# A small input as 128 rows of 64 bytes, its statistics by matmul, and a query picked by a register, in a decode block with grouped-query attention

## The chip, the cores and the metric

The kernel runs on one core of a Trainium2 chip. Its time is the device time of one execution in microseconds. A core has five engines with instruction streams of their own: TensorE (PE, matrix multiplications into PSUM), VectorE (DVE), ScalarE (ACT), GpSimd (POOL) and SyncE (SP). They meet only by semaphores. Transfers between the main memory and the on-chip memory (SBUF, 128 partitions) are done by 16 DMA engines. SP and ACT each issue transfers into a DMA queue of their own; in the profile queue 1 is SP's and queue 10 is ACT's. A transfer that has landed raises a semaphore by 16.

## The reference

One token (a decode step) for a batch of two. The input is normalized, and the result is the input plus an attention over a long cache plus a feed-forward layer, both of the normalized input. Everything is 32-bit floating point.

```python
B, Sq, D = 2, 1, 1024
Hq, Hkv, Sk, Dh = 32, 4, 32768, 128
F = 3584

xn = (x - mean(x)) / sqrt(var(x) + 1e-5)          # over the last axis, 1024 numbers
q  = (xn @ wq) -> 32 heads of 128                 # wq 1024 x 4096
k, v = caches (2, 4, 32768, 128), each head used by 8 query heads
o  = softmax(q k^T * 128**-0.5) v
A  = o @ wo                                       # wo 4096 x 1024
Bf = silu(xn @ w1) @ w2                           # w1 1024 x 3584, w2 3584 x 1024
out = x + A + Bf
```

The caches are 268 MB of the 331 MB that are read; the weights are the rest.

## The kernel before, in words

All large operands stream through two buffers of 8 MiB, `bufA` and `bufB` (128 partitions of 64 KB). SP issues the loads in a fixed order, alternating the buffers: `wq[0]`, `wq[1]`, `w1b`, `w1a`; then for each of 8 turns (4 key heads by 2 batch entries) the two halves of the keys `kt` and the two halves of the values `v0`, `v1`; then `wo[0]`, `wo[1]`, `w2a`, `w2b`. Ahead of a load SP waits until TensorE has finished with the buffer's last content: the semaphore `freed`, which VectorE raises in `relay` (line 199) when TensorE's progress count `turn_sem` says so. The `load` helper is at line 167.

Each buffer's content is multiplied by TensorE as 32 groups of matmuls with weights of 32 columns from a small tile `wtA` or `wtB` (line 107 records all matmuls). TensorE runs one loop over pairs of buffers (`te_loop`, `te_more`, line 372 on). Before it uses a buffer it takes two tokens: `ld`, that the buffer has landed, and `tok`, that the small weight tile is ready. Between the pairs it does small matmuls that the softmax needs: with a matrix of ones it sums over partitions, with the identity it transposes.

The start is this. SP issues `wq[0]` (line 110). GpSimd clears the tile `xs` (line 113) and one large tile `blank` (line 114), out of which several smaller tiles are cut that have to begin as zeros. After the first clearing ACT issues the transfer `x8` into `xs` (line 116): 8 rows of 4 KB, the two input rows in four rotations, on every sixteenth partition. After the second it issues `x`, 4 rows of 2 KB, into `xres` (line 118): the residual that is added at the end. SP waits for `x8` to land (line 119, semaphore `ldx`), then issues `wq[1]` (line 120). VectorE takes mean and variance with its statistics instructions (lines 139 to 143), the reciprocal of the square root with one square root on ACT and a Newton step (lines 146 to 151), normalizes 256 columns and transposes them in blocks of 32 (lines 152 and 153) into `xT`. ACT spreads `xT` over `wtA` and GpSimd over `wtB` (lines 161 to 164); with these TensorE can begin `wq[0]`.

The query vectors come out of `wq` and lie in `tqs`. In each turn ACT copies the 8 query columns of that turn into `qcur` (`query`, line 226), GpSimd clears the weight tile and places them in it (`stage`, line 296), the keys are multiplied, VectorE finds the maxima and subtracts them (`attend`, line 259), ACT takes exponentials into the weight tiles (line 236), the values are multiplied, and the normalized result `onew` is copied by ACT into `oT` (line 238); the next copy into `qcur` follows it. VectorE and GpSimd run their 8 turns as a loop with a register as counter (lines 309 to 317).

At the end GpSimd sums partial results and the residual `xres` (lines 334 to 340; the wait for the residual's landing is at line 335), TensorE adds the last pieces of `w2b` one by one as they land, ACT copies the sum out of PSUM (line 246) and SP stores it (line 345).

```python
sp.dma_start(buf[0], wq[0]).then_inc(ld[0], 16)
...
A.dma_start(xs[::16, :], x8).then_inc(ldx, 16)
act.wait(z)
A.dma_start(xres[0:64:16, :], x).then_inc(ldr, 16)
sp.wait_ge(ldx, 16)
sp.dma_start(buf[1], wq[1]).then_inc(ld[1], 16)
```

Of the kernel before, what the change touches and what calls it, by code (L numbers as in the profile page):

```python
# [5 lines left out]
ALU = mybir.AluOpType  # L6
AX = mybir.AxisListType

B, HQ, HKV, SK, DH, D, F = 2, 32, 4, 32768, 128, 1024, 3584
P = 128  # L10
REP = HQ // HKV
W = 16384
NC = SK // W
KT = D // P
FT = F // P
QW = D // 4
CUT = 3 * QW // 4
LOOPS = HKV * B
STEPS = 4 + 4 * LOOPS + 4
PAIRS = STEPS // 2  # L20
EPS = 1e-5
# [27 lines left out]
        self.eng.sem_inc(token, -n)  # L49


def gqa_plus_mlp_kernel(nc, x, x8, kt, v0, v1, wq, wo, w1a, w1b, w2a, w2b, out):


    pe, dve, act, pool = (Stream(nc, e, n) for e, n in
                          ((nc.tensor, "pe"), (nc.vector, "dve"), (nc.scalar, "act"), (nc.gpsimd, "pool")))
    sp, T, V, A, G = nc.sync, nc.tensor, nc.vector, nc.scalar, nc.gpsimd
# [6 lines left out]
    def sb(name, *shape):  # L64
        return nc.alloc_sbuf_tensor(name, shape, F32).ap()
# [5 lines left out]
    ld, more, tok = ([sem(f"{n}{k}") for k in "AB"] for n in ("ld", "more", "tok"))  # L71
    ldx, ldr, done, turn_sem, self_sem = (sem(n) for n in ("ldx", "ldr", "done", "marks", "self"))
    freed, subbed, normed, tq, pself = (sem(n) for n in ("freed", "subbed", "normed", "tq", "pself"))
    trm, tgd, tls, tob = (sem(n) for n in ("trm", "tgd", "tls", "tob"))
    last = [sem(f"last{i}") for i in range(5)]

    wt = [sb(n, P, 32, 32) for n in ("wtA", "wtB")]
    st = [sb(f"st{c}", P, 1024) for c in range(NC)]
    xs, xT = sb("xs", P, D), sb("xT", P, KT, 32)
    stats, mv, ln = sb("stats", P, 2, V.BN_STATS_DIM), sb("mv", P, 2), sb("ln", P, 6)  # L80
    ev = [sb(f"ev{i}", P, 1024) for i in range(4)]
    sums = [sb(f"sum{i}", P, 512) for i in range(4)]
    tqs = [sb(f"tq{i}", P, 16, 32) for i in range(2)]
    pre, sig, rsig = sb("pre", P, FT, 32), sb("sig", P, FT, B), sb("rsig", P, FT, B)
    qcur, onew = sb("qcur", P, REP), sb("onew", P, REP)
    ones = sb("ones", P, P)
    blank, used = sb("blank", P, P + 32 + 160 + 3 * REP + 1024 + 32 * (HQ + FT)), [0]

    def zeroed(*shape):
        n = shape[0] * (shape[1] if len(shape) > 1 else 1)  # L90
        lo = used[0]
        used[0] += n
        t = blank[:, lo:lo + n]
        return t.rearrange("p (a m) -> p a m", m=shape[1]) if len(shape) > 1 else t

    ident, sel, fold, rm, lsum, gd, ob, xres = (zeroed(n) for n in (P, 32, 160, REP, REP, REP, 512, 512))
    oT, hT = zeroed(HQ, 32), zeroed(FT, 32)
    rest, ob1, ot = sb("rest", P, 512), sb("ob1", P, 512), sb("ot", P, QW)
    mx, ls = sb("mx", P, NC, REP), sb("ls", P, NC, REP)
    gm, gmax, rl = sb("gm", REP, 1), sb("gmax", P, 1, REP), sb("rl", P, REP)  # L100
# [2 lines left out]
    smA, smB = bank("smA"), bank("smB")  # L103
    acc = bank("acc")[:, :QW]

    def mm(o, lhsT, rhs, start=True, stop=True):
        return T.matmul(o, lhsT, rhs, start=start, stop=stop)  # L107
# [2 lines left out]
    sp.dma_start(buf[0], wq[0]).then_inc(ld[0], 16)  # L110


    z_x = pool.mark(G.memset(xs, 0.0))
    z = pool.mark(G.memset(blank, 0.0))
    act.wait(z_x)
    A.dma_start(xs[::16, :], x8).then_inc(ldx, 16)
    act.wait(z)
    A.dma_start(xres[0:64:16, :], x).then_inc(ldr, 16)
    sp.wait_ge(ldx, 16)
    sp.dma_start(buf[1], wq[1]).then_inc(ld[1], 16)  # L120

# [1 line left out]
    t = pool.mark(G.affine_select(out=ident, in_=ident, compare_op=ALU.not_equal, fill=1.0, base=0,  # L123
                                  pattern=[[-1, P]], channel_multiplier=1))
    pool.wait(t)
    halves = fold[:, 32:].rearrange("p (a m) -> p a m", m=64)[:, :, :32]
    t = pool.mark(G.tensor_add(halves, *(ident[:, 64 * g:64 * g + 64].rearrange("p (a m) -> p a m", m=32)
                                         for g in range(2))))
    pool.wait(t)
    G.tensor_add(sel, halves[:, 0], halves[:, 1]).then_inc(tob, 1)  # L130
    t = pool.mark(G.memset(ones, 1.0))
    pool.pass_on(tls, 1, t)
    for s in (trm, tgd):
        G.sem_inc(s, 1)
    for s in more:
        G.sem_inc(s, 16 * (PAIRS - 1))


    dve.wait((ldx, 16))
    for i in range(2):  # L140
        t = dve.mark(V.bn_stats(stats[:, i, :], xs[:, i * 512:(i + 1) * 512]))
    dve.wait(t)
    t = dve.mark(V.bn_aggr(mv, stats))
    var, std, y0, t0, t1, rstd = (ln[:, i:i + 1] for i in range(6))
    dve.wait(t)
    t = dve.mark(V.tensor_scalar_add(var, mv[:, 1:2], EPS))
    act.wait(t)
    t = act.mark(A.activation(std, var, AF.Sqrt))
    for f in (lambda: V.reciprocal(y0, std), lambda: V.tensor_mul(t0, y0, y0), lambda: V.tensor_mul(t1, t0, var),
              lambda: V.tensor_scalar(t0, t1, -0.5, 1.5, op0=ALU.mult, op1=ALU.add),  # L150
              lambda: V.tensor_mul(rstd, y0, t0),
              lambda: V.tensor_scalar(xs[:, :256], xs[:, :256], mv[:, 0:1], rstd, op0=ALU.subtract, op1=ALU.mult),
              lambda: V.transpose(xT.rearrange("p k m -> p (k m)"), xs[:, :256])):
        dve.wait(t)
        t = dve.mark(f())
    i_xT = t

    def spread_x(copy, to):
        return copy(to.rearrange("p (k q) m -> p k q m", q=4), xT[:, :, None, :].to_broadcast([P, KT, 4, 32]))

    act.wait(i_xT)
    spread_x(A.copy, wt[0]).then_inc(tok[0], 1)
    pool.wait(i_xT)
    spread_x(G.tensor_copy, wt[1]).then_inc(tok[1], 1)


    def load(k, dst, src, s, n):
# [7 lines left out]
    for it in range(LOOPS):  # L175
        h, b = divmod(it, B)
# [12 lines left out]
    for n in range(4):  # L189
        act.wait((freed, n + 1))  # L190
        t = act.mark(A.copy(ev[n], ps[n % 2]))  # L191
# [10 lines left out]
    relay(2)  # L202
    for n in range(2):
        dve.wait(read[n])
        i_q = dve.mark(V.transpose(tqs[n].rearrange("p c m -> p (c m)"), sums[n]))  # L205
    relay(5)
    relay(6)
    dve.wait(read[2])
# [4 lines left out]
    t = dve.mark(V.transpose(pre[:, :16].rearrange("p t m -> p (t m)"), sums[3]))  # L213

    act.wait(t)
    t = act.mark(A.activation(sig, pre[:, :, ::16], AF.Exp, scale=-1.0))
    for f in (lambda: V.tensor_scalar_add(sig, sig, 1.0), lambda: V.reciprocal(rsig, sig),
              lambda: V.tensor_mul(hT[:, :, ::16], pre[:, :, ::16], rsig)):
        dve.wait(t)
        t = dve.mark(f())  # L220
# [2 lines left out]
    V.sem_inc(turn_sem, -8)  # L223


    def query(it):
        h, b = divmod(it, B)
        A.copy(qcur, tqs[h // 2][:, REP * (h % 2):REP * (h % 2) + REP, 16 * b]).then_inc(tq, 1)

    act.wait(i_q)  # L230
    query(0)
    for it in range(LOOPS):
        h, b = divmod(it, B)
        for c in range(NC):
            act.wait((subbed, NC * it + c + 1))
            A.activation(wt[c].rearrange("p e m -> p (e m)"), st[c], AF.Exp, scale=SCALE).then_inc(tok[c], 1)  # L236
        act.wait((normed, it + 1))
        i_oT = act.mark(A.copy(oT[:, REP * h:REP * (h + 1), 16 * b], onew))  # L238
        if it + 1 < LOOPS:
            query(it + 1)  # L240
    outs = []
    for n in range(3):
        act.wait((freed, STEPS - 3 + n))
        outs.append(act.mark(A.copy(ev[n], ps[n % 2])))
    act.wait((pe, 2))
    i_ot = act.mark(A.copy(ot, acc))  # L246


# [10 lines left out]
    def attend():  # L259
# [33 lines left out]
        V.sem_inc(self_sem, -at[0])  # L293
        V.sem_inc(turn_sem, -8)

    def stage():
        G.wait_ge(tq, 1)
        G.sem_inc(tq, -1)  # L298
        for c in range(NC):
            G.memset(wt[c], 0.0).then_inc(pself, 1)  # L300
            G.wait_ge(pself, c + 1)
            for a in range(2):
                o = bass.AP(tensor=wt[c].tensor, offset=wt[c].offset + 512 * a,
                            ap=[wt[c].ap[0], [136, 4], [32, 4], [1, REP]])
                m = G.tensor_copy(o, qcur[:, None, None, :].to_broadcast([P, 4, 4, REP]))
            m.then_inc(tok[c], 1)
        G.sem_inc(pself, -2)

    turns = [(V, attend, V.alloc_register("ve_turn")), (G, stage, G.alloc_register("po_turn"))]
    for eng, f, reg in turns:  # L310
        eng.reg_mov(reg, 0)
        eng.br("turns")
    with nc.body("turns", valid_engines=[V.engine, G.engine]):
        for eng, f, reg in turns:
            f()
            eng.reg_add(reg, reg, 1)
            eng.br_lt(reg, LOOPS, on_true="turns", on_false="after")
    nc.switch_bb("after")
    for n in (1, 2, 5):
        relay(n)  # L320

    for c in range(NC):
        if c == 0:
            pool.wait(i_oT)
        G.tensor_copy(wt[c].rearrange("p (t d) m -> p t d m", d=2),
                      oT[:, 16 * c:16 * c + 16, None, :].to_broadcast([P, 16, 2, 32])).then_inc(tok[c], 1)
    for s in (trm, tgd):
# [4 lines left out]
        G.tensor_copy(wt[c][:, :2 * n].rearrange("p (t d) m -> p t d m", d=2),  # L332
                      hT[:, 16 * c:16 * c + n, None, :].to_broadcast([P, n, 2, 32])).then_inc(tok[c], 1)
    t = pool.mark(G.tensor_add(ev[0], ev[0], ev[1]))
    pool.wait(t, (ldr, 16))
    t = pool.mark(G.tensor_add(ev[0][:, :512], ev[0][:, :512], xres))
    pool.wait(t, outs[2])
    t = pool.mark(G.tensor_add(ev[0], ev[0], ev[2]))
    pool.wait(t)
    t = pool.mark(G.tensor_add(rest, ev[0][:, :512], ev[0][:, 512:]))  # L340
    dve.wait(t, (pe, 1))
    V.tensor_add(ob, rest, ps[1][:, :512]).then_inc(tob, 1)  # L342

    sp.wait_ge(act.sem, i_ot[1])
# [51 lines left out]
    with nc.body("te_far", valid_engines=engine):  # L396
        T.reg_mov(pair, 0)
        T.reg_mov(half, 0)
        T.br("te_loop")
    nc.switch_bb("te_rest")  # L400

# [62 lines left out]
```

## Time and profile before

| | |
|---|---|
| time, median of 3 runs | 773.19 us (773.11 to 773.69) |
| profiled execution | 772.86 us, of which the span between first and last instruction is 771.6 us |
| read from main memory | 331.39 MB, 430 GB/s over the span |
| busy: PE, DVE, ACT, POOL | 386.7, 142.4, 30.9, 45.0 us |
| SP's queue (1) | 6928 packets, 331.37 MB |
| ACT's queue (10) | 24 packets, 0.04 MB |

Busy times are sums over an engine's instructions. Waiting, issuing a transfer and register work are not counted. The profile also lists for each queue the packets that the DMA engines moved (a packet is one contiguous piece, or the few bytes that raise a semaphore), for each issue the time until its data had landed, and for each wait what ended it. Time that an engine idles matters only where the end of the program hangs on it.

### The profile page before, as it was taken

How to read it: one execution, taken by the hardware profiler on the slowest of the kernel's cores; microseconds unless marked ns; L12 is line 12 of the kernel's file. 1: busy time of each engine (PE TensorE's matmuls, PEld its weight loads, DVE VectorE, ACT ScalarE, POOL GpSimd, SP SyncE). 2: the span in 40 equal slices, each digit the busy share in tenths (PEclk: the TensorE clock that was granted, in tenths of full speed). 3: DMA queues.
4: the chain of work that ended last, by engine and by line, in shares of the span. 5: the costliest groups of instructions: out<-in, count | busy, mean ns of one | idle time of the engine just before them, and what ended most of it. 6: DMA issues, size and time to landing. Idle time of an engine off the chain costs nothing. (4 is left out here: it accounts for less than half of the span.)

```text
span 771.6 us, 6137 instructions
## 1 busy us (share of the span) xinstructions
PE 386.7 (50%) x2702; PEld 120.1 (16%) x2702; DVE 142.4 (18%) x174; ACT 30.9 (4%) x45; POOL 45.0 (6%) x71
## 2 busy tenths in 40 slices
PE   0454554464555454554464555454554464555476
PEld 0111111121111111111121111111111121111122
DVE  1000113111311131113111311131113111311000
ACT  1000101000100010001000100000001000000000
POOL 3000200010001000100000001000100000001021
PEclk9977767767767767767767767767767767767789
DMA  9999999999999999999999999999999999999997
GB/s 384 435 435 435 435 435 435 435 435 435 435 435 435 435 435 435 435 435 435 435 431 435 431 435 435 435 435 435 435 431 428 425 425 428 425 435 435 435 435 327
DMA packets 6954, 331.44 MB, mean 430 GB/s; under 512 B 780, under 2 KB 924, under 8 KB 1448
## 3 DMA queue, kind: packets, MB, share of 16 engines
q1 hardware_dynamic: 6928, 331.37, 99.4%
q10 hardware_dynamic: 24, 0.04, 0.0%
q8 instruction: 1, 0.02, 0.0%
q14 instruction: 1, 0.01, 0.0%
HBM read 331.39 MB, written 0.02 MB: 430 GB/s over the span
## 5 line engine op out<-in xcount | busy, mean ns | idle before, releaser
L107 PE MATMUL xy<-bufB,wtB 128*32 128x512 f32 x1248 | 177.7, 733 | 196.5 <-PEq L49 196.5
L107 PE MATMUL xy<-bufA,wtA 128*32 128x512 f32 x1280 | 182.4, 733 | 118.7 <-PEq L49 118.7
L107 PEld LDWEIGHTS xy<-bufB,wtB 128*32 128x32 f32 x1248 | 48.9, 132 | 325.3 <-issue 325.2
L107 PEld LDWEIGHTS xy<-bufA,wtA 128*32 128x32 f32 x1280 | 50.1, 132 | 234.6 <-issue 234.6
L262 DVE STREAM_TRANSPOSE st<-xy 128x1024 f32<-128x1024 f32 x16 | 20.0, 1250 | 237.1 <-PE xy L107 237.1
L300 POOL MEMSET wtA<- 128x1024 f32 x8 | 7.6, 951 | 525.7 <-POOLq L298 525.7
L264 DVE TENSOR_REDUCE mx<-st 128x8 f32<-128x1024 f32 x16 | 31.7, 1980 | 0.6
L283 DVE TENSOR_TENSOR ob<-ob,xy 128x512 f32<-128x512 f32 x8 | 5.5, 687 | 127.8 <-PE xy L107 127.8
L277 DVE COPY ob<-xy 128x512 f32<-128x512 f32 x8 | 5.5, 691 | 93.1 <-PE xy L107 93.1
L236 ACT ACTIVATE wtA<-st 128x1024 f32<-128x1024 f32 x8 | 8.5, 1057 | 315.7 <-DVE st L275 315.7
L107 PE MATMUL smA<-blank 128*8 128x128 f32 x20 | 4.2, 295 | 30.3 <-PEq L49 30.3
L107 PE MATMUL smA<-blank,ones 128*128 128x8 f32 x18 | 3.9, 288 | 30.6 <-PEq L49 30.6
L275 DVE TENSOR_TENSOR st<-st,gmax 128x1024 f32<-128x1024 f32 x16 | 18.9, 1220 | 0.3
L280 DVE TENSOR_REDUCE ls<-wtA 128x8 f32<-128x1024 f32 x8 | 15.8, 1972 | 0.0
L286 DVE TENSOR_REDUCE ls<-wtB 128x8 f32<-128x1024 f32 x8 | 15.8, 1972 | 0.0
L238 ACT COPY blank<-onew 128x8 f32<-128x8 f32 x8 | 1.6, 204 | 285.3 <-DVE onew L292 285.3
L107 PE MATMUL smB<-blank 128*128 128x8 f32 x72 | 12.3, 299 | 0.0
L107 PEld LDWEIGHTS smB<-blank 128*128 128x128 f32 x72 | 11.8, 248 | 0.0
L342 DVE TENSOR_TENSOR blank<-rest,xy 128x512 f32<-128x512 f32 x1 | 0.7, 687 | 55.5 <-PE acc L107 55.5
L107 PEld LDWEIGHTS smA<-blank,ones 128*128 128x128 f32 x18 | 3.3, 229 | 38.5 <-issue 38.5
L196 POOL TENSOR_TENSOR sum<-ev 128x512 f32<-128x512 f32 x4 | 5.0, 1260 | 67.7 <-ACT ev L191 67.7
L205 DVE STREAM_TRANSPOSE tq<-sum 128x512 f32<-128x512 f32 x2 | 1.4, 712 | 39.2 <-PE xy L107 37.5
(63 smaller groups left out, 98.4 us busy)
## 6 DMA issues: line engine op xcount, KB each, us to landing
bufA<-in_w2a SPq DMA_DIRECT2D x2, 4096.0 KB, 24.2
bufA<-in_w1b SPq DMA_DIRECT2D x1, 6144.0 KB, 25.0
bufB<-in_w2b SPq DMA_DIRECT2D x1, 3072.0 KB, 16.7
bufB<-in_w2b SPq DMA_DIRECT2D x3, 512.0 KB, 20.4
bufB<-in_w2b SPq DMA_DIRECT2D x1, 1024.0 KB, 18.8
bufB<-in_w2b SPq DMA_DIRECT2D x1, 384.0 KB, 21.7
bufA<-in_kt SPq DMA_DIRECT2D x8, 29.2
bufB<-in_kt SPq DMA_DIRECT2D x8, 29.1
```

The source lines that it names most:

```text
L107: return T.matmul(o, lhsT, rhs, start=start, stop=stop)
L196: read.append(pool.mark(G.tensor_add(sums[n], ev[n][:, :512], ev[n][:, 512:])))
L236: A.activation(wt[c].rearrange("p e m -> p (e m)"), st[c], AF.Exp, scale=SCALE).then_inc(tok[c], 1)
L238: i_oT = act.mark(A.copy(oT[:, REP * h:REP * (h + 1), 16 * b], onew))
L262: t = mine(V.transpose(st[c], ps[c]))
L264: t = mine(V.tensor_reduce(mx[:, c, :], e8[c].rearrange("p n m -> p m n"), AX.X, ALU.max))
L275: V.tensor_sub(e8[c], e8[c], gmax.to_broadcast([P, 128, REP])).then_inc(subbed, 1)
L277: t = mine(V.tensor_copy(ob1, ps[0][:, :512]))
L280: mine(V.tensor_reduce(ls[:, 0, :], w8[0], AX.X, ALU.add))
L283: t = mine(V.tensor_add(ob1, ob1, ps[1][:, :512]))
L286: t = mine(V.tensor_reduce(ls[:, 1, :], w8[1], AX.X, ALU.add))
L300: G.memset(wt[c], 0.0).then_inc(pself, 1)
```

## The change

- **The input.** `x8` and the clearing of `xs` go. The input comes as `xk`, 128 rows of 64 bytes, one row for each partition (8 numbers of each of the two batch entries). ACT issues it as its first instruction, without a wait. SP still waits for it ahead of `wq[1]`.
- **Mean and variance.** VectorE sums each partition's 8 numbers; TensorE multiplies with a matrix of ones, which gives the sum over partitions on every partition. The mean is subtracted, the squares are summed in the same way, and the reciprocal square root follows as before, now on two columns. The result goes straight into `xT`, which is now part of `blank`. GpSimd spreads `xT` over both weight tiles.
- **The query.** ACT copies all query columns once into `qall`, in the order of the turns. GpSimd's `stage` reads its 8 columns at a place given by its loop register, which now steps by 8. Its signal in each turn is the copy into `oT`.
- **The residual.** It comes in three transfers of 128, 128 and 256 columns with 10, 12 and 14 rows; in the prepared array the 4 rows of the residual stand at rows 0, 2, 4 and 6, and the others are zero. The wait counts to 48.
- TensorE's progress count `pe` starts two higher, so the later waits on it do too.

```diff
-    z_x = pool.mark(G.memset(xs, 0.0))
+    A.dma_start(xs.rearrange("p k b -> p (k b)"), xk).then_inc(ldx, 16)
     z = pool.mark(G.memset(blank, 0.0))
-    act.wait(z_x)
-    A.dma_start(xs[::16, :], x8).then_inc(ldx, 16)
+    i_ones = pool.mark(G.memset(ones, 1.0))
     act.wait(z)
-    A.dma_start(xres[0:64:16, :], x).then_inc(ldr, 16)
+    for lo, hi, n in ((0, 128, 10), (128, 256, 12), (256, 512, 14)):
+        A.dma_start(xres[:8 * n:8, lo:hi], x[:n, lo:hi]).then_inc(ldr, 16)
     sp.wait_ge(ldx, 16)
     sp.dma_start(buf[1], wq[1]).then_inc(ld[1], 16)
...
     dve.wait((ldx, 16))
-    for i in range(2):
-        t = dve.mark(V.bn_stats(stats[:, i, :], xs[:, i * 512:(i + 1) * 512]))
...
+    i_s1 = dve.mark(V.tensor_reduce(s1, xs.rearrange("p k b -> p b k"), AX.X, ALU.add))
+    dve.wait((pe, 1))
+    t = dve.mark(V.scalar_tensor_tensor(xc, wide(smA[:, :B]), -1.0 / D, xs, op0=ALU.mult, op1=ALU.add))
+    for f in (lambda: V.tensor_mul(sq, xc, xc),
+              lambda: V.tensor_reduce(s2, sq.rearrange("p k b -> p b k"), AX.X, ALU.add)):
+        dve.wait(t)
+        t = dve.mark(f())
+    i_s2 = t
+    dve.wait((pe, 2))
+    t = dve.mark(V.tensor_scalar(var, smB[:, :B], 1.0 / D, EPS, op0=ALU.mult, op1=ALU.add))
...
+    dve.wait(t)
+    i_xT = dve.mark(V.tensor_mul(xT[:, :, ::16], xc, wide(t1)))
...
-    act.wait(i_xT)
-    spread_x(A.copy, wt[0]).then_inc(tok[0], 1)
     pool.wait(i_xT)
-    spread_x(G.tensor_copy, wt[1]).then_inc(tok[1], 1)
+    for k in range(2):
+        spread_x(G.tensor_copy, wt[k]).then_inc(tok[k], 1)
...
-    def query(it):
-        h, b = divmod(it, B)
-        A.copy(qcur, tqs[h // 2][:, REP * (h % 2):REP * (h % 2) + REP, 16 * b]).then_inc(tq, 1)
-
     act.wait(i_q)
-    query(0)
+    A.copy(qall.rearrange("p (h b) m -> p h b m", b=B),
+           tqs[:, :, ::16].rearrange("p (h m) b -> p h b m", m=REP)).then_inc(tq, 1)
...
     def stage():
-        G.wait_ge(tq, 1)
-        G.sem_inc(tq, -1)
+        pool.take(tq)
+        q = qall.rearrange("p i m -> p (i m)")[:, bass.ds(G.snap(at_q), REP)]
...
-                m = G.tensor_copy(o, qcur[:, None, None, :].to_broadcast([P, 4, 4, REP]))
+                m = G.tensor_copy(o, q[:, None, None, :].to_broadcast([P, 4, 4, REP]))
...
-    pool.wait(t, (ldr, 16))
+    pool.wait(t, (ldr, 48))
...
+        pe.wait(i_ones, i_s1)
+        pe.mark(mm(smA[:, :B], ones, s1))
+        pe.wait(i_s2)
+        pe.mark(mm(smB[:, :B], ones, s2))
         T.br("te_loop")
```

More of the change, by code (lines that the diff above doesn't have):

```diff
@@ L49, in take, with gqa_plus_mlp_kernel @@
         self.eng.sem_inc(token, -n)
-def gqa_plus_mlp_kernel(nc, x, x8, kt, v0, v1, wq, wo, w1a, w1b, w2a, w2b, out):
+def gqa_plus_mlp_kernel(nc, xk, x, kt, v0, v1, wq, wo, w1a, w1b, w2a, w2b, out):
     pe, dve, act, pool = (Stream(nc, e, n) for e, n in
@@ L78, in gqa_plus_mlp_kernel @@
     st = [sb(f"st{c}", P, 1024) for c in range(NC)]
-    xs, xT = sb("xs", P, D), sb("xT", P, KT, 32)
-    stats, mv, ln = sb("stats", P, 2, V.BN_STATS_DIM), sb("mv", P, 2), sb("ln", P, 6)
+    xs, xc, sq = (sb(n, P, KT, B) for n in ("xs", "xc", "sq"))
+    ln = sb("ln", P, 7, B)
     ev = [sb(f"ev{i}", P, 1024) for i in range(4)]
     sums = [sb(f"sum{i}", P, 512) for i in range(4)]
-    tqs = [sb(f"tq{i}", P, 16, 32) for i in range(2)]
+    tqs, qall = sb("tqs", P, 32, 32), sb("qall", P, LOOPS, REP)
     pre, sig, rsig = sb("pre", P, FT, 32), sb("sig", P, FT, B), sb("rsig", P, FT, B)
-    qcur, onew = sb("qcur", P, REP), sb("onew", P, REP)
+    onew = sb("onew", P, REP)
     ones = sb("ones", P, P)
-    blank, used = sb("blank", P, P + 32 + 160 + 3 * REP + 1024 + 32 * (HQ + FT)), [0]
+    blank, used = sb("blank", P, P + 32 + 160 + 3 * REP + 1024 + 32 * (KT + HQ + FT)), [0]
     def zeroed(*shape):
@@ L96, in gqa_plus_mlp_kernel @@
     ident, sel, fold, rm, lsum, gd, ob, xres = (zeroed(n) for n in (P, 32, 160, REP, REP, REP, 512, 512))
-    oT, hT = zeroed(HQ, 32), zeroed(FT, 32)
+    xT, oT, hT = zeroed(KT, 32), zeroed(HQ, 32), zeroed(FT, 32)
     rest, ob1, ot = sb("rest", P, 512), sb("ob1", P, 512), sb("ot", P, QW)
@@ L130, in gqa_plus_mlp_kernel @@
     G.tensor_add(sel, halves[:, 0], halves[:, 1]).then_inc(tob, 1)
-    t = pool.mark(G.memset(ones, 1.0))
-    pool.pass_on(tls, 1, t)
-    for s in (trm, tgd):
+    for s in (tls, trm, tgd):
         G.sem_inc(s, 1)
@@ L136, in gqa_plus_mlp_kernel @@
         G.sem_inc(s, 16 * (PAIRS - 1))
+    s1, s2, var, std, y0, t0, t1 = (ln[:, i] for i in range(7))
+    wide = lambda t: t[:, None, :].to_broadcast([P, KT, B])
     dve.wait((ldx, 16))
-    for i in range(2):
[L141 to L146, printed above, removed]
+    i_s1 = dve.mark(V.tensor_reduce(s1, xs.rearrange("p k b -> p b k"), AX.X, ALU.add))
[8 more added lines that the diff above has]
+    t = dve.mark(V.tensor_scalar(var, smB[:, :B], 1.0 / D, EPS, op0=ALU.mult, op1=ALU.add))
     act.wait(t)
@@ L150, in gqa_plus_mlp_kernel @@
               lambda: V.tensor_scalar(t0, t1, -0.5, 1.5, op0=ALU.mult, op1=ALU.add),
-              lambda: V.tensor_mul(rstd, y0, t0),
-              lambda: V.tensor_scalar(xs[:, :256], xs[:, :256], mv[:, 0:1], rstd, op0=ALU.subtract, op1=ALU.mult),
-              lambda: V.transpose(xT.rearrange("p k m -> p (k m)"), xs[:, :256])):
+              lambda: V.tensor_mul(t1, y0, t0)):
         dve.wait(t)
         t = dve.mark(f())
-    i_xT = t
+    dve.wait(t)
+    i_xT = dve.mark(V.tensor_mul(xT[:, :, ::16], xc, wide(t1)))
     def spread_x(copy, to):
         return copy(to.rearrange("p (k q) m -> p k q m", q=4), xT[:, :, None, :].to_broadcast([P, KT, 4, 32]))
-    act.wait(i_xT)
-    spread_x(A.copy, wt[0]).then_inc(tok[0], 1)
     pool.wait(i_xT)
-    spread_x(G.tensor_copy, wt[1]).then_inc(tok[1], 1)
+    for k in range(2):
+        spread_x(G.tensor_copy, wt[k]).then_inc(tok[k], 1)
     def load(k, dst, src, s, n):
@@ L204, in gqa_plus_mlp_kernel @@
         dve.wait(read[n])
-        i_q = dve.mark(V.transpose(tqs[n].rearrange("p c m -> p (c m)"), sums[n]))
+        i_q = dve.mark(V.transpose(tqs[:, 16 * n:16 * n + 16].rearrange("p c m -> p (c m)"), sums[n]))
     relay(5)
@@ L237, in gqa_plus_mlp_kernel @@
         act.wait((normed, it + 1))
-        i_oT = act.mark(A.copy(oT[:, REP * h:REP * (h + 1), 16 * b], onew))
-        if it + 1 < LOOPS:
-            query(it + 1)
+        A.copy(oT[:, REP * h:REP * (h + 1), 16 * b], onew).then_inc(tq, 1)
     outs = []
@@ L244, in gqa_plus_mlp_kernel @@
         outs.append(act.mark(A.copy(ev[n], ps[n % 2])))
-    act.wait((pe, 2))
+    act.wait((pe, 4))
     i_ot = act.mark(A.copy(ot, acc))
@@ L294, in attend @@
         V.sem_inc(turn_sem, -8)
+    at_q = G.alloc_register("at_q")
     def stage():
-        G.wait_ge(tq, 1)
-        G.sem_inc(tq, -1)
+        pool.take(tq)
+        q = qall.rearrange("p i m -> p (i m)")[:, bass.ds(G.snap(at_q), REP)]
         for c in range(NC):
@@ L304, in stage @@
                             ap=[wt[c].ap[0], [136, 4], [32, 4], [1, REP]])
-                m = G.tensor_copy(o, qcur[:, None, None, :].to_broadcast([P, 4, 4, REP]))
+                m = G.tensor_copy(o, q[:, None, None, :].to_broadcast([P, 4, 4, REP]))
             m.then_inc(tok[c], 1)
         G.sem_inc(pself, -2)
-    turns = [(V, attend, V.alloc_register("ve_turn")), (G, stage, G.alloc_register("po_turn"))]
-    for eng, f, reg in turns:
+    turns = [(V, attend, V.alloc_register("ve_turn"), 1), (G, stage, at_q, REP)]
+    for eng, f, reg, step in turns:
         eng.reg_mov(reg, 0)
@@ L313, in gqa_plus_mlp_kernel @@
     with nc.body("turns", valid_engines=[V.engine, G.engine]):
-        for eng, f, reg in turns:
+        for eng, f, reg, step in turns:
             f()
-            eng.reg_add(reg, reg, 1)
-            eng.br_lt(reg, LOOPS, on_true="turns", on_false="after")
+            eng.reg_add(reg, reg, step)
+            eng.br_lt(reg, step * LOOPS, on_true="turns", on_false="after")
     nc.switch_bb("after")
@@ L323, in gqa_plus_mlp_kernel @@
         if c == 0:
-            pool.wait(i_oT)
+            G.wait_ge(tq, 1)
         G.tensor_copy(wt[c].rearrange("p (t d) m -> p t d m", d=2),
@@ L340, in gqa_plus_mlp_kernel @@
     t = pool.mark(G.tensor_add(rest, ev[0][:, :512], ev[0][:, 512:]))
-    dve.wait(t, (pe, 1))
+    dve.wait(t, (pe, 3))
     V.tensor_add(ob, rest, ps[1][:, :512]).then_inc(tob, 1)
@@ L426, in lay @@
         return np.ascontiguousarray(np.asarray(a).reshape(shape).transpose(order)).reshape(to)
-    xr = np.asarray(A_x).reshape(B, D)
+    x_ = np.asarray(A_x).reshape(B, D)
+    spaced = np.zeros((14, 512), x_.dtype)
+    spaced[:8:2] = lay(x_, (B, 2, 512), (1, 0, 2), (4, 512))
     v = np.asarray(A_v_cache).reshape(B, HKV, NC, W, DH)
@@ L441 @@
     arrays = {
-        "x": np.ascontiguousarray(xr.reshape(B, 2, 512).transpose(1, 0, 2)).reshape(4, 512),
-        "x8": np.stack([np.roll(xr, -QW * g, axis=1) for g in range(4)]).reshape(8, D),
+        "xk": lay(x_, (B, 4, KT, 32), (1, 3, 2, 0), (P, KT * B)),
+        "x": spaced,
         "kt": lay(A_k_cache, (B, HKV, NC, W, DH), (0, 1, 2, 4, 3), (B, HKV, NC, P, W)),
```

## The prediction

> **What bounds the kernel now.** I read first the page's slices, queues and chain, then the waits of SP's DMA queue, then the order of time at the start.
>
> ```profile
> span 771.6 us, 6137 instructions
> GB/s 384 435 435 435 435 435 435 435 435 435 435 435 435 435 435 435 435 435 435 435 431 435 431 435 435 435 435 435 435 431 428 425 425 428 425 435 435 435 435 327
> DMA packets 6954, 331.44 MB, mean 430 GB/s; under 512 B 780, under 2 KB 924, under 8 KB 1448
> q1 hardware_dynamic: 6928, 331.37, 99.4%
> q10 hardware_dynamic: 24, 0.04, 0.0%
> q8 instruction: 1, 0.02, 0.0%
> DMA 3%; PE 2%; SPq 0%; ACT 0%; issue 0%; DVEq 0%
> bufA<-in_kt SPq DMA_DIRECT2D x8, 29.2
> bufA<-in_wq SPq DMA_DIRECT2D x1, 22.5
> bufB<-in_wq SPq DMA_DIRECT2D x1, 31.7
> ...
> SPq L170 <- DVEq L44: 719.7, 38, 21.0
> SPq L120 <- DMA xs<-in_x: 9.8, 1, 9.8
> ```
>
> Queue 1, SP's bulk transfers, holds the 16 DMA engines for 99.4% of the span. The slices run at 435 GB/s except the first, the last and a few at 421 to 431, so the kernel is a transfer of 331 MB with a start and an end around it. An 8 MiB load takes 8.39 MB / 435 GB/s = 19.3 us, but from issue to landing a load of `kt` takes 29.2 us: it is queued 29.2 - 19.3 = 9.9 us ahead of need. SP's long wait of 719.7 us costs nothing for that reason. An edit matters if it makes a bulk load late by more than this cover, or if it touches the start or the end.
>
> The start, in order of time (start us, length us, engine, line), then the DMA queues cut into short windows. In each window the GB/s line has 40 slices, a number is what began in that slice, and a queue row is packets, MB, share.
>
> ```profile
> 0.74 0.37 SPq L110 DMA_DIRECT2D bufA<-in_wq  x1
> 1.71 1.15 ACTq L116 DMA_DIRECT2D xs<-in_x  x1
> 4.49 0.53 ACTq L118 DMA_DIRECT2D blank<-in_x  x1
> 10.90 0.33 SPq L120 DMA_DIRECT2D bufB<-in_wq  x1
> 10.91 1.29 DVE L141 BATCH_NORM_STATS2 stats<-xs 128x6 f32<-128x512 f32 x2 [10.91 <-DMA xs<-in_x]
> 14.79 1.04 ACT L159 COPY wtA<-xT 128x1024 f32<-128x1024 f32 x1 [1.93 <-DVE xT L153]
> 14.82 1.04 POOL L159 COPY wtB<-xT 128x1024 f32<-128x1024 f32 x1 [8.96 <-DVE xT L153]
> 23.55 8.59 PE L107 MATMUL xy<-bufA,wtA 128*32 128x512 f32 x64 [23.55 <-PEq L49]
> 32.25 0.68 SPq L170 DMA_DIRECT2D bufA<-in_w1b  x1
> 42.90 9.15 PE L107 MATMUL xy<-bufB,wtB 128*32 128x512 f32 x64 [10.76 <-PEq L49]
> ```
>
> Windows 0 to 4.6 us (its GB/s line), 7 to 9.6 us, 9.6 to 12 us (their queue rows), and 21.8 to 23 us (its GB/s line):
>
> ```profile
> GB/s 0 0 0 0 0 0 0 0 0 0 0 0 0 0 0 2849 2992 570 1710 570 0 0 0 0 570 0 0 0 0 0 0 0 0 0 0 0 0 0 0 0
> ...
> q1 hardware_dynamic: 16, 1.05, 93.7%
> q10 hardware_dynamic: 8, 0.03, 3.1%
> ...
> q1 hardware_dynamic: 16, 1.05, 101.2%
> q10 hardware_dynamic: 8, 0.00, 0.2%
> ...
> GB/s 0 2185 4369 0 0 0 4369 0 6554 4369 0 2185 2185 2185 0 2185 0 0 0 0 0 0 0 0 0 0 0 2185 0 0 0 0 0 2185 0 0 0 0 0 0
> ```
>
> A window of some 2.5 us holds 16 packets of queue 1 with 1.05 MB, so 64 KB each, one per engine: `wq[0]` (128 rows of 64 KB) is 8 such rounds. Queue 10 is ACT's. `x8` (8 rows) appears there as 8 data packets in one round (0.03 MB) and 8 semaphore packets (0.00 MB) in the next, though a semaphore packet is tiny. So while `wq[0]` is in the rings, queue 10 gets **one packet per engine and round**, even for packets of one transfer. That is why 32 KB issued at 1.71 us releases SP only at 10.90 us. It costs nothing today: the last round of `wq[0]` ends between 21.83 us (slice 1 of the last line, 0.03 us each) and 22.82 us (slice 34), and `wq[1]` has been queued since 10.90 us, so there is no gap.
>
> **The change, part by part.**
>
> *x as 128 rows of 64 bytes.* ACT issues it first, without the memset it waited for, so about 0.7 to 1.3 us into the span, level with `wq[0]`. Like `wq[0]`, 128 rows are 8 per engine, and a semaphore makes 9 packets where `x8` had 2. If each needs a turn beside 64 KB packets, they last as long as the 8 rounds of `wq[0]`: with the first row in front of the first bulk packet, row 8 follows bulk packet 7 and the semaphore follows packet 8; if the first rows miss a turn, the remainder passes when `wq[0]` is through. Both ways x lands with `wq[0]`, at 0.74 + 22.5 = 23.24 us, not 10.9. SP keeps its wait ahead of `wq[1]`, so this load, and all SP's loads behind it, move.
>
> Price of the hole: SP issues `wq[1]` at about 23.3 us. After the issue of `wq[0]` at 0.74 us the first packets began at slice 15 of 0.115 us, 1.73 us, and 15 of 16 by slice 19, 2.2 to 2.3 us; so `wq[1]`'s begin at 23.3 + 1.0 = 24.3 us, and by 24.8 us. Before, its rounds began from 21.83 to 22.82 us. The first engines thus start 24.3 - 21.83 = 2.5 us later and the last ones 24.8 - 22.82 = 2.0 us. A queue that starts may also pay on its first packet:
>
> ```profile
> 1.70:4.70 3.00, 0.00 (x0) 0.00 (x0) 0.00 (x0) 0.00 (x0) 2.76 (x2) 1.00 1.04 355
> 4.70:7.10 2.40, 0.00 (x0) 0.00 (x0) 0.00 (x0) 1.28 (x1) 1.00 (x4) 1.00 1.01 437
> ```
>
> The first round moved 3.00 x 355 = 1065 KB, at 437 GB/s 2.44 us, so it lost 0.56 us. A second start loses between 0 and that. The floor is an engine that was last and is now among the first, 24.3 - 22.82 = 1.5 us; the ceiling 2.5 + 0.56 = 3.1 us. The last engine with the excess gives 2.0 + 0.56 = 2.6, the first without it 2.5: I take **+2.5 us**.
>
> *Mean and variance by matmuls.* Rows for its pieces:
>
> ```profile
> L107 PE MATMUL smA<-blank,ones 128*128 128x8 f32 x18 | 3.9, 288 | 30.6 <-PEq L49 30.6
> L107 PEld LDWEIGHTS smA<-blank,ones 128*128 128x128 f32 x18 | 3.3, 229 | 38.5 <-issue 38.5
> L288 DVE TENSOR_REDUCE blank<-ls 128x8 f32<-128x16 f32 x8 | 1.4, 171 | 0.3
> ```
>
> Removed: from 10.91 to 14.79 us, 3.9 us. Added: two matmul passes of about 0.23 + 0.29 plus hand-offs, 0.7 us each; about eleven VectorE operations on at most 16 elements at about 0.17 to 0.2 us, 2.1 us; one square root, 0.2 us: 3.7 us, with one hand-off more at each end some 4.5 us. GpSimd then copies both weight tiles one after the other, 1.04 us each, where ACT and GpSimd did one each; the second is needed only for `wq[1]`. If x lands at 23.3 us, the first tile is ready at 23.3 + 4.5 + 1.0 = 28.8 us instead of waiting from 15.8 us. PE then starts on `wq[0]` 5.3 us later than its 23.55 us and frees the buffer near 37.5, not 32.25 us. Cover: `wq[1]` lands 22.5 us or less after its issue at 23.3, about 45 us, so `w1b` is still queued some 7 us ahead. Cost 0; if that cover were gone, every further us would be paid. If x lands early all of this lies before 23.55 us, cost 0.
>
> *Query by register.* ACT's copy of the query goes, GpSimd's five operations per buffer stay, with a register added to their addresses.
>
> ```profile
> 144.25 0.33 SPq L170 DMA_DIRECT2D bufA<-in_kt  x1
> 170.63 0.20 ACT L238 COPY blank<-onew 128x8 f32<-128x8 f32 x1 [37.27 <-DVE onew L292]
> 170.74 0.20 ACT L228 COPY qcur<-tq 128x8 f32<-128x8 f32 x1
> 171.09 0.95 POOL L300 MEMSET wtA<- 128x1024 f32 x1 [78.17 <-POOLq L298]
> ```
>
> GpSimd starts up to 0.2 us earlier per turn. Keys issued at 144.25 us land near 173.4 us, so first weights at about 172.7 us are just in time, and a register that cost a microsecond would make PE late but meet the 9.9 us of cover: 0 either way. Only above that would it be paid, eight times.
>
> *Residual in three transfers.* 36 rows (10 + 12 + 14) instead of 4, of 512 B to 1 KB. From the 8 packets of `x8` (3.1% of 16 x 2.6 us) a 4 KB packet costs 0.16 us and a semaphore (0.2% of 16 x 2.4 us) 0.01 us; three smaller ones with their semaphores cost an engine at most 0.5 us, at least 0.03. They stand behind x in ACT's ring, so they pass in the hole or beside bulk packets; `x8`'s own 0.16 us goes. Net -0.2 to +0.3 us, taken as 0. The sum that needs them:
>
> ```profile
> 748.66 1.26 POOL L336 TENSOR_TENSOR ev<-ev,blank 128x512 f32<-128x512 f32 x1
> ```
>
> It runs at 748.66 us, hundreds of us after they land. The end (last `w2b` piece, PE, ACT, output) is not edited.
>
> Sum: the profiled execution took 772.86 us (span 771.6), the runs' median is 773.19; +2.5 on the median is **775.7 us**. The three runs spread over 0.58 us, and 0.2% (1.55 us) is about what a measurement can tell from no change.
>
> **The rivals.**
>
> *Rows of one transfer pass together.* If an engine drains x's eight short rows in one turn, x lands in the second or third round, by 10.9 us as `x8` did or sooner, `wq[1]` is queued before 11 us, and nothing is left but the -0.2 to +0.3 us: 773.2. Against it: `x8`'s semaphore did not pass with its data. For it: no engine had two data rows of one transfer in queue 10, so rows following rows are not shown. It decides as soon as x lands before about 20.5 us (21.83 less 1.0 from issue to packet and 0.3 to wake SP). The Trainium skill, in "DMA: Bandwidth & Descriptors", section "Queues, rings and completion order", states that each engine goes round-robin between queues at packet granularity and drains a whole packet, typically 9 to 17 descriptors, before it switches. By that rule, nine descriptors in one packet would pass in one turn and the time would be this rival's 773.2; the split of `x8`'s data and semaphore speaks against a packet that spans them.
>
> *x is through before `wq[0]` arrives.* ACT waits for nothing now. If its nine short packets are in the rings half a microsecond before the bulk ones, x lands near 3 us: 773.1. Against it: ACT's issues took 0.53 and 1.15 us, SP's 0.37.
>
> *Faster.* An engine that carried `x8` and the old residual loses at most about 0.16 us for the 4 KB packet, 0.08 for one of half its bytes and 0.02 for two semaphores; with the instruction packet of queue 8 falling elsewhere in the start, a last engine might gain 1 us (the spread of 21.83 to 22.82). Both together are 1.3 us, 771.9, still within 0.2%; it takes something at the end as well.
>
> **How the numbers follow.** Hole at `wq[1]`: 0.62, 774.7 to 776.3 (1.5 to 3.1 above). Rows together: 0.22. Through first: 0.10. Faster or a mixture with a gain: 0.06. The hole passes 1.55 us except at its floor, about 0.92 of its chance, 0.57; with 0.01 for costs not seen, slower is 0.58; same 0.36; faster 0.06. The range runs from 772.5, for the early cases with a small gain, to 776.4.
>
> **What would show it.** Right: SP's wait for x near 22 us instead of 9.8, DVE's first operation near 23.4 us, first bulk load into `bufB` issued near 23.3 us, a slice without queue-1 packets between 22.8 and 24.3 us, queue 10 with 8 or 16 packets in each early window, PE's first matmul on `wq[0]` near 29 us, everything after it shifted by the same 2.5 us. Wrong: that wait under 20 us, or a DMA share without a gap there. A turn's PE start moved against its keys' landing, with `w1b` or `kt` issued under 1 us ahead of need, would show a cover that I held for safe.

## The result, and the profile after

The changed kernel takes 776.17 us (median of 7 runs, 775.97 to 776.31); the kernel before, on the same chip, 773.23 us. The ratio is 1.0037, with a 95% interval of 1.0025 to 1.0049: slower by 2.94 us. The forecast was 775.7.

The page of the changed kernel, the lines that answer to those shown of before:

```profile
span 774.6 us, 6196 instructions
GB/s 380 380 413 454 433 433 433 433 433 433 433 433 433 433 433 433 433 433 433 433 433 433 433 433 433 433 433 433 433 433 433 433 433 433 433 433 433 433 432 328
DMA packets 7146, 331.43 MB, mean 428 GB/s; under 512 B 948, under 2 KB 1128, under 8 KB 1640
q1 hardware_dynamic: 6928, 331.37, 99.1%
q10 hardware_dynamic: 216, 0.03, 0.0%
```

The span grew by 3.0 us with the same 6928 packets in SP's queue. The stream has a new low place in the second slice (380 instead of 435 GB/s: a slice is 774.6 / 40 = 19.4 us, so this one runs from 19.4 to 38.7 us); from the fifth slice to the last but one it is as steady as before. (Bytes are counted where a packet begins, so 413 and 454 in the third and fourth slice are to be read together: their mean is 433.5.) ACT's queue has 216 packets: 128 rows and 16 semaphores of x, 36 rows and 36 semaphores of the residual.

The start of the changed kernel in order of time:

```profile
0.74 0.37 SPq L110 DMA_DIRECT2D bufA<-in_wq  x1
0.74 0.40 ACTq L113 DMA_DIRECT2D xs<-in_xk  x1
...
23.68 0.33 SPq L120 DMA_DIRECT2D bufB<-in_wq  x1
23.68 0.17 DVE L140 TENSOR_REDUCE ln<-xs 128x2 f32<-128x16 f32 x1 [23.68 <-DMA xs<-in_xk]
...
27.53 1.04 POOL L161 COPY wtA<-blank 128x1024 f32<-128x1024 f32 x1 [22.48 <-DVE blank L158]
28.50 1.04 POOL L161 COPY wtB<-blank 128x1024 f32<-128x1024 f32 x1
28.71 9.87 PE L107 MATMUL xy<-bufA,wtA 128*32 128x512 f32 x64 [2.89 <-PEq L49]
38.70 0.68 SPq L171 DMA_DIRECT2D bufA<-in_w1b  x1
```

x was issued at 0.74 us, a microsecond earlier than before, and landed 13 us later. SP's wait for it, 9.8 us before, is now:

```profile
SPq L120 <- DMA xs<-in_xk: 22.6, 1, 22.6
```

In the windows 7.2 to 9.6 us and 9.6 to 12 us the queues (packets, MB, share) show why:

```profile
q1 hardware_dynamic: 16, 1.05, 100.8%
q10 hardware_dynamic: 16, 0.00, 0.5%
...
q1 hardware_dynamic: 16, 1.05, 100.8%
q10 hardware_dynamic: 16, 0.00, 0.5%
```

Sixteen 64 KB packets of SP and sixteen packets of ACT in each round: on every DMA engine one row of 64 bytes, then one of 64 KB. Eight rows and the semaphore so last as long as `wq[0]`. What follows is the hole. First the bulk stream before, then after, both in the window 21.6 to 29.6 us (0.2 us a slice, bytes counted where a packet begins):

```profile
GB/s 0 983 3277 328 0 328 328 0 0 0 0 0 0 983 2621 983 0 328 328 0 0 0 0 0 0 983 2621 983 0 328 328 0 0 0 0 0 0 983 2621 983
```

```profile
GB/s 0 35 69 22 0 0 0 8 0 0 0 0 0 0 0 3277 655 655 655 0 0 0 0 0 0 0 0 0 0 0 1311 1638 1966 0 328 0 0 0 0 0
```

Before, the rounds begin in slices 1 to 6, 13 to 18, 25 to 30: every 2.4 us. After, slices 1 to 7 hold only small packets (ACT's, and the sixteen semaphore packets of `wq[0]`); the first round of `wq[1]` begins in slices 15 to 18 (24.6 to 25.4 us) and the next in slices 30 to 34, 3.0 us later. So the new first round begins 2.4 to 2.8 us late and lasts some 0.6 us longer than a round in the flow. A table by stage of the changed kernel (window, length, busy time of the five engines, clock, DMA share, GB/s) says the same:

```profile
21.80:24.60 2.80, 0.56 (x2) 0.50 (x2) 0.18 (x2) 0.00 (x0) 0.00 (x0) 1.00 0.04 10
24.60:27.60 3.00, 0.58 (x2) 0.50 (x2) 1.67 (x10) 0.20 (x1) 0.07 (x1) 1.00 1.04 350
27.60:30.00 2.40, 1.29 (x8) 0.45 (x12) 0.00 (x0) 0.00 (x0) 1.95 (x2) 1.00 1.01 437
```

For 2.8 us the DMA engines moved next to nothing (share 0.04, 10 GB/s); then a round took 3.0 us. The 3 us are carried to the end: in the chain that ended last, the wait for the last `w2b` piece ends at 745.88 + 20.41 = 766.29 us before and at 747.87 + 21.45 = 769.32 us after, 3.0 us apart.

```profile
745.88 20.41 DMA bufB<-in_w2b
```

```profile
747.87 21.45 DMA bufB<-in_w2b
...
769.35 2.27 PE acc L107 x20
771.62 0.00 issue
771.62 0.69 PE acc L107 x16
```

### The profile page after: what moved, and what is told of

Read it like the earlier page. It is cut to its first block, busy times and chain, and to the rows that moved or that the text cites. A ratio compares the mean times of both kernels' runs of the same rounds, so it can differ in the third digit from the quotient of the medians.

```text
span 774.6 us, 6196 instructions
## 1 busy us (share of the span) xinstructions
PE 393.7 (51%) x2706; PEld 122.8 (16%) x2706; DVE 141.0 (18%) x174; ACT 29.2 (4%) x37; POOL 45.4 (6%) x71
## 3 DMA queue, kind: packets, MB, share of 16 engines
q1 hardware_dynamic: 6928, 331.37, 99.1%
## 5 line engine op out<-in xcount | busy, mean ns | idle before, releaser
L107 PE MATMUL xy<-bufB,wtB 128*32 128x512 f32 x1248 | 179.8, 740 | 190.9 <-PEq L49 190.9
L107 PE MATMUL xy<-bufA,wtA 128*32 128x512 f32 x1280 | 185.8, 745 | 95.6 <-PEq L49 95.6
L234 ACT ACTIVATE wtB<-st 128x1024 f32<-128x1024 f32 x8 | 8.4, 1056 | 0.6
## 6 DMA issues: line engine op xcount, KB each, us to landing
bufA<-in_w1b SPq DMA_DIRECT2D x1, 6144.0 KB, 21.6
```

## The experiments

The theory of the hole: x needs nine turns beside 64 KB packets, and SP's wait for it keeps `wq[1]` out of the rings until `wq[0]` has drained. The rivals: the time is lost in the other parts of the change, or it grows with the number of small packets.

**The wait taken away (e1).**

```diff
-    sp.wait_ge(ldx, 16)
     sp.dma_start(buf[1], wq[1]).then_inc(ld[1], 16)
```

> The changed kernel, but SP no longer waits for x ahead of wq[1]. Theory of the hole (x's eight rows and its semaphore need nine turns beside the 64 KB packets, and SP's wait for them leaves the queue empty after wq[0]): the hole at 22 to 25 us goes, x lands one round later, near 25.5 us, because its ninth turn now stands beside wq[1]. In the changed kernel w1b is issued 15.0 us after x is there (38.70 - 23.68), so here near 41 us with first packets near 42 us, while wq[1] ends between 41.2 and 42.2 us: the cover is just used up, 773.2 to 774.5 us. Rival (the time is lost in the other parts: matmuls for the statistics, the late first matmul, the query by register): the wait is innocent and the time stays at 776.2 us.

Measured: 773.49 us against 773.16 for the kernel before, ratio 1.0005 (0.9996 to 1.0014). The loss is gone, though all other parts of the change are in this kernel and x lands only 0.5 us earlier than in the changed kernel. Its start:

```profile
1.17 0.42 SPq L119 DMA_DIRECT2D bufB<-in_wq  x1
...
23.18 0.17 DVE L139 TENSOR_REDUCE ln<-xs 128x2 f32<-128x16 f32 x1 [23.18 <-DMA xs<-in_xk]
...
37.32 0.68 SPq L170 DMA_DIRECT2D bufA<-in_w1b  x1
```

One step of the expectation missed: x landed at 23.2 us, not near 25.5. The order of the packets in this run's trace shows why: on fifteen of the sixteen engines the eighth row is followed by `wq[0]`'s own semaphore packet, then x's, then the first packet of `wq[1]`, all within 0.02 us. The ninth turn stood beside a semaphore packet, which costs almost nothing. So the cover for `w1b` was not used up either: `w1b` was issued at 37.32 us, while `wq[1]` landed near 1.17 + 41.5 = 42.7 us.

**The rows alone, in the kernel before (e2).** `spare` is a new tile, `ldk` a semaphore of its own.

```diff
     sp.dma_start(buf[0], wq[0]).then_inc(ld[0], 16)
+    A.dma_start(spare, xk).then_inc(ldk, 16)
...
     sp.wait_ge(ldx, 16)
+    sp.wait_ge(ldk, 16)
     sp.dma_start(buf[1], wq[1]).then_inc(ld[1], 16)
```

> The kernel before, with one thing added: ACT first issues the 128 rows of 64 bytes into a spare tile, and SP waits for them as well ahead of wq[1]. Statistics, query and residual are as before. Theory of the hole: x8 stands behind the 128 rows in ACT's ring and both land with wq[0], SP is released near 23.7 us, the whole loss appears: 776.2 us (775.5 to 776.6). Rival (other parts): 773.3 us, since none of them is in this kernel.

Measured: 775.70 us, ratio 1.0033 (1.0021 to 1.0045), 2.54 us above the kernel before. One transfer of 8 KB, which nothing but SP uses, makes most or all of the loss, with the statistics, the query and the residual of before. (`x8` stands behind it in ACT's queue and is late as well: VectorE began on it at 22.98 us, 0.6 us before SP was released at 23.59 us.) Its wait of SP's queue, and the bulk stream in the window 21.6 to 29.6 us, with the same hole:

```profile
SPq L122 <- DMA spare<-in_xk: 22.4, 1, 22.4
...
GB/s 42 95 73 1 0 0 0 0 0 0 0 0 0 0 983 3604 328 0 0 0 328 0 0 0 0 0 0 0 0 0 983 3277 983 0 0 0 0 0 0 0
```

**Fewer rows: five, six and seven per engine (e3, e7, e5).** The number n is 80, 96, 112. ACT issues x 0.14 us later than in the changed kernel (0.88 us), behind GpSimd's short clearing.

```diff
-    A.dma_start(xs.rearrange("p k b -> p (k b)"), xk).then_inc(ldx, 16)
+    z_x = pool.mark(G.memset(xs.rearrange("p k b -> p (k b)"), 0.0))
+    act.wait(z_x)
+    A.dma_start(xs.rearrange("p k b -> p (k b)")[:n], xk[:n]).then_inc(ldx, 16)
```

> The changed kernel with only the first 80 rows of x loaded, five per DMA engine instead of eight; the other 48 partitions are left at zero (GpSimd clears the small tile first, some 0.2 us), so part of the input is left out and the output is not the reference's. Theory of the hole: five rows and a semaphore are six turns, the semaphore passes by 18.3 us on the last engine, SP is released near 18.7 us, its first packets could begin near 19.7 us, two microseconds before wq[0] is through: no hole, 773.2 us (772.9 to 773.6). Rival (the loss grows with the number of small packets): 60% of the loss stays, 775.0 us.

> As with 80 rows, but the first 96 rows of x, six per DMA engine; the other 32 partitions stay zero, so part of the input is left out and the output is not the reference's. Theory of the hole: the semaphore has the seventh turn, 19.4 us on the first engines and 20.7 us on the last; SP is released near 21.1 us and its first packets could begin near 22.1 us, when the first engines have been idle for 0.3 us and the last are still in wq[0]: the edge of the hole, 773.2 to 773.9 us. Rival (loss grows with the number of rows): 75% of it, 775.4 us.

> As with 96 rows, but 112 rows, seven per DMA engine; the other 16 partitions stay zero, so part of the input is left out and the output is not the reference's. Theory of the hole: the semaphore's turn is the one behind the eighth bulk packet, so SP is released within 0.1 us of the changed kernel's 23.68 us and the whole loss is there: 776.1 us (775.6 to 776.5). One row per engine more than with 96 rows would so cost 2 us or more, and the eighth row nothing. Rival (loss grows with the number of rows): 775.8 us with 96 rows at 775.4 us, a step of 0.4 us.

SP's wait for x, with 80, 96 and 112 rows:

```profile
SPq L122 <- DMA xs<-in_xk: 17.5, 1, 17.5
```

```profile
SPq L122 <- DMA xs<-in_xk: 19.6, 1, 19.6
```

```profile
SPq L122 <- DMA xs<-in_xk: 22.4, 1, 22.4
```

| rows per engine | SP's wait, us | time, us | above before (773.16) |
|---|---|---|---|
| 5 (e3) | 17.5 | 773.21 (ratio 0.9992 to 1.0010) | 0.05 |
| 6 (e7) | 19.6 | 774.50 (1.0008 to 1.0027) | 1.34 |
| 7 (e5) | 22.4 | 775.91 (1.0022 to 1.0049) | 2.75 |
| 8 (the change) | 22.6 | 776.17 (1.0025 to 1.0049) | 2.94 (on 773.23) |

A row more is a turn more, 2.1 to 2.8 us of waiting, and the eighth adds 0.2 us. The time does not follow the number of rows: five of eight cost nothing that can be told, seven cost what eight do. The place of the step is where the theory puts it. Six rows missed: the expectation had 773.2 to 773.9, it was 774.50, and single runs ranged from 773.14 to 775.11 us. The bulk stream of that kernel in the window 21.6 to 29.6 us shows what the expectation lacked:

```profile
GB/s 5 707 1987 1682 328 335 0 328 0 0 0 0 0 0 0 655 1638 1311 655 655 0 0 0 328 0 0 0 0 1966 1638 655 655 0 0 0 328 0 0 0 0
```

`wq[1]`'s first round begins in slices 1 to 7, hardly later than before (1 to 6): there is almost no hole. But the next round begins in slices 15 to 23, and the one after in slices 28 to 35. The first round took about 2.8 us or more (for the last engine 3.2), the next one about 2.5. A first packet that reaches its engine just as the engine runs dry thus pays for its start even with almost no hole ahead of it.

These lines also show which engine the time follows. Each engine carries its own eight rows of such a load, and the load has landed when the last engine is through. The last packet of `wq[1]`'s second round begins in slice 18 before, 34 in the changed kernel, 32 in e2 and 23 with six rows, so 3.2, 2.8 and 1.0 us late. The spans are 3.0, 2.8 and 1.2 us longer than the 771.6 us of before (774.6, 774.4, 772.8). With six rows the first packet of that round is only 2 slices late (0.4 us): one late engine made most of this loss.

**The rows twice (e6).**

```diff
     A.dma_start(xs.rearrange("p k b -> p (k b)"), xk).then_inc(ldx, 16)
+    A.dma_start(spare, xk).then_inc(ldk, 16)
...
     sp.wait_ge(ldx, 16)
+    sp.wait_ge(ldk, 16)
```

> The changed kernel with a second transfer of the same 128 rows into a spare tile behind the first, and SP waiting for both. Theory of the hole: the second transfer's rows find queue 1 empty after wq[0] and pass without waiting for a turn, 9 packets of 0.02 to 0.04 us, so SP's wait ends 0.2 to 0.4 us later than in the changed kernel: 776.3 to 776.7 us. Rival (a price per small packet, or a turn beside something else for every packet): twice the loss, 779 us or more.

Measured: 776.59 us, ratio 1.0044 (1.0030 to 1.0057), 3.43 us above the kernel before. Twice the packets do not cost twice the loss, and the time lies in the range expected:

```profile
SPq L122 <- DMA spare<-in_xk: 22.6, 1, 22.6
```

The expected mechanism is only in part there. The wait is as long as in the changed kernel, and SP was released at 23.81 us, 0.13 us later, not 0.2 to 0.4. The medians are 0.4 to 0.5 us apart, within their intervals, and both profiled spans are 774.6 us; so whether the second transfer costs anything is not shown.

**x ahead of the stream (e4).**

```diff
-    sp.dma_start(buf[0], wq[0]).then_inc(ld[0], 16)
-    A.dma_start(xs.rearrange("p k b -> p (k b)"), xk).then_inc(ldx, 16)
+    A.dma_start(xs.rearrange("p k b -> p (k b)"), xk).then_inc(ldx, 16)
+    act.pass_on(sent, 1)
+    sp.wait_ge(sent, 1)
+    sp.dma_start(buf[0], wq[0]).then_inc(ld[0], 16)
```

> The changed kernel, but SP issues wq[0] only after ACT has issued x (ACT signals right behind its issue, which took 0.40 us). Nothing else differs. Theory of the hole: x's packets are in the rings before any 64 KB packet, none has to wait for a turn, x lands by 4 us; wq[0] is issued near 1.2 us instead of 0.74 us, so the stream starts about 0.45 us later, and no hole follows: 773.6 us (773.3 to 774.1), 2.6 us better than the changed kernel. Rival (small packets lose by themselves, or the other parts cost): 776 us or more, since wq[0] also starts later.

Measured: 773.38 us, ratio 1.0003 (0.9994 to 1.0012). The same 128 rows behind the same wait, 0.45 us earlier than `wq[0]`, land at 3.9 us and cost nothing that can be told:

```profile
0.74 0.39 ACTq L111 DMA_DIRECT2D xs<-in_xk  x1
1.19 0.37 SPq L114 DMA_DIRECT2D bufA<-in_wq  x1
...
3.88 0.33 SPq L123 DMA_DIRECT2D bufB<-in_wq  x1
```

None of the kernels is faster than the kernel before; e1 and e4 are level with it, and so is e3, which leaves out part of the input. Against the changed kernel e1 and e4 repair the loss.

## Why the prediction was right, point by point

**The bound and the place.** The stream of bulk loads bounds the kernel, and only its start was touched: shown by the GB/s lines and by e1 and e2, which take the loss away and bring it with the wait and the rows alone.

**One packet per engine and round.** Right. The step rested on one data packet and one semaphore; the changed kernel shows it for rows behind rows, 16 and 16 in each window, and the table of five to eight rows counts the turns. With that, the rival that rows pass together has fallen. Of the two orders that the prediction left open the second came: the first rows missed a turn, and the remainder passed when `wq[0]` was through. That is why seven rows cost what eight do. The Trainium skill ("DMA: Bandwidth & Descriptors", section "Queues, rings and completion order") has the engines go round-robin between queues at packet granularity, with typically some 9 to 17 descriptors to a packet. The trace agrees with the turns, but not with that size: a packet here held a single row, or nine of them would have passed at once.

**The price of the hole.** The mechanism was right, and the sum 0.4 us short (2.5 forecast, 2.94 measured; 776.17 us is 0.2 us inside the upper end of the range). Two terms were too small. SP was released at 23.68 us, not 23.3. The last engine was through `wq[0]` 0.3 us later than before, and x's last packet passed there at 23.1 us (slice 7 of the changed kernel's line from 21.6 us on); SP issued some 0.6 us after it. In e3 and e7 it was 0.5 us from x's last packet (18.17 and 20.27 us) to SP's issue. The 0.3 us for waking SP, which the prediction used for its limit of 20.5 us, stands in no row. With the later release the new round began at 24.6 to 25.4 us, not 24.3 to 24.8. And the excess of a first packet, held between 0 and 0.56 us and taken for the last engine only, was there in full: the first round moved 350 GB/s in 3.0 us, against 437 GB/s in the flow, an excess of 0.6 us like the kernel's very first round. The span follows the engine that is last: 2.4 us late and 0.6 us for its first packet make 3.0 us, and the span grew by 3.0. The prediction had this path at 2.0 + 0.56 = 2.6 us; the 2.5 us that it took were those of the first engines without the excess, which did not bind.

**Statistics by matmul.** The first matmul was forecast near 28.8 us and came at 28.71 us, by two errors that offset each other: x was 0.4 us later than forecast, and from x to the first weight tile it took 28.57 - 23.68 = 4.9 us, not 4.5 + 1.0 = 5.5. `w1b` was forecast for 37.5 us and came at 38.70 us, since TensorE's pass took 9.87 us, not 8.59. The cover held: `wq[1]` landed at 23.68 + 22.0 = 45.7 us, 7.0 us later. Cost 0, as far as can be told: e1, whose first matmul comes nearly as late (28.22 us), is level with the kernel before.

**Query by register.** Cost 0, as forecast, but the time under the cover moved the other way. A turn of the kernel before, then one of the changed kernel:

```profile
170.63 0.20 ACT L238 COPY blank<-onew 128x8 f32<-128x8 f32 x1 [37.27 <-DVE onew L292]
...
172.10 0.52 POOL L305 COPY wtA<-qcur 128x128 f32<-128x128 f32 x2
```

```profile
171.63 0.20 ACT L236 COPY blank<-onew 128x8 f32<-128x8 f32 x1 [34.38 <-DVE onew L288]
172.06 0.95 POOL L298 MEMSET wtA<- 128x1024 f32 x1 [74.88 <-POOLq L49]
173.41 0.52 POOL L303 COPY wtA<-qall 128x128 f32 x2 [0.39 <-POOL wtA L298]
...
176.65 9.30 PE L107 MATMUL xy<-bufA,wtA 128*32 128x512 f32 x64 [5.49 <-PEq L49]
```

From ACT's copy to GpSimd's first copy of the query it was 172.10 - 170.63 = 1.47 us and is now 173.41 - 171.63 = 1.78 us. ACT's copy of 0.2 us is gone, but GpSimd idles 0.39 us ahead of the first operation with the register's address. That the register is the cause was not tested. TensorE began on these keys only at 176.65 us, 2.7 us after that copy ended, so nothing of it is paid.

**Residual.** Taken as 0. Its 72 packets passed in the hole or beside bulk packets; e1 and e4 carry them and are within 0.2 to 0.3 us of the kernel before, inside their intervals.

**x through first.** It did not happen: both issues began at 0.74 us, and on fifteen of the sixteen engines a 64 KB packet was first. (In the window 0 to 4.6 us the trace has sixteen packets of queue 1 and one of queue 10.) e4 shows that the rival's reasoning held, with 0.45 us enough.

**Still open.** The rows alone cost 2.54 us and the whole change 2.94; e1, the rest without the hole, is 0.33 us above the kernel before. The two fit, but each interval reaches 0.7 to 0.9 us to either side, so whether the other parts cost these 0.3 us or nothing is not settled.

## What to carry to other kernels

A small transfer beside a saturated stream is priced by its packets per DMA engine, not its bytes: each waited for one bulk packet here, so 8 KB in 128 rows landed 13 us later than 32 KB in 8 rows. That alone cost nothing that could be told (e1). It cost 2.5 to 2.9 us when SP waited for it ahead of the next bulk load, and that load missed the end of the one before. Look for such a wait ahead of a bulk load, and either take it away or issue the small transfer ahead of the stream (0.45 us were enough in e4); both gave the time back here. Judge a late load by its last DMA engine, not by the average.

## What the runs showed of the hardware that was not expected

- A transfer that starts on dry engines pays about 0.6 us on its first round (3.0 us for 64 KB packets instead of 2.4), even 22 us into a stream and after a gap of under 3 us, and with 96 rows 0.4 to 0.8 us with almost no gap. Why the first packet takes longer, no run here shows. A load that is queued ahead of time does not show this: before, the first round of `wq[1]` followed and ended in the rhythm of 2.4 us.
- The semaphore packets of the bulk queue count as turns as well: without SP's wait x landed at 23.2 us, behind `wq[0]`'s semaphore packets, though its ninth turn was expected behind a further 64 KB packet, 2.4 us later.
- In the turn shown, the first GpSimd operation whose address comes from a register began 0.39 us after the operation ahead of it had ended; before, with a constant address, 172.10 - (171.09 + 0.95) = 0.06 us.
